# A one-core attention and two-layer feed-forward kernel: the issue order planned with row-weighted TensorE columns and six jittered replays

## The chip, the cores and the metric

The kernel runs on one core of a Trainium2 chip. The metric is the device time of one execution in microseconds (us). The kernel before takes 739.07 us, the median of three executions (737.53, 739.07 and 739.49). One more execution was taken with the hardware profiler on, and all rows below come from that one.

## What is computed

All inputs are float32 (the layer weights reach the kernel as 64-bit floats). The attention has 4 batches, 8 heads, 576 positions and head size 64. Heads 0 to 3 see a local band, heads 4 to 7 a stride of 32:

```
rel = pos[:, None] - pos[None, :]
mask_local = (rel >= 0) & (rel < 32)
mask_strided = (rel >= 0) & (pos[None, :] % 32 == pos[:, None] % 32)
attn = softmax(where(mask, q @ k.T / sqrt(64), -1e9)) @ v
x = attn reshaped to 2304 tokens x 512
h = x @ w_in                              # 512 x 1024
s = h * softmax(h)
x = (s - mean(s)) / sqrt(var(s) + 1e-6) * g_ln @ w_out    # 1024 x 512
out = ((x @ w_a) * (x @ w_b)) @ w_out2    # 512 x 1536, 1536 x 512
```

## The kernel before, in words

**Stages.** The kernel has three kinds of work on the five engines. *Attention*: 40 tiles, 10 for each batch. For a tile TensorE (PE) makes the scores (`scores`, lines 706 and 709), VectorE (DVE) takes the row maxima, subtracts them and sums the exponentials (722, 731, 735, 740), ScalarE (ACT) does the exponential (734), GpSimd (POOL) divides (784), and PE multiplies by V (`pv`, line 803 for batch 0, lines 808 to 810 for the others). `group_T` (line 615) transposes q and k on PE (624). The score products contract over 64 rows of the PE array, the others over 54 to 128. *First layer*: 18 token tiles of 128 (`moe1`, line 838), each 24 matmuls of 512 columns into `h` (861) and then a chain on DVE (854, 866, 869, 890), ACT and POOL; each pair of tiles ends in `s2` (line 903), 96 matmuls of 256 columns into `y` (910). The weights are first converted from 64-bit floats on ACT and DVE (`from_f64`, lines 468, 470, 475, 481) and split into two 16-bit halves (`split_wout`, 548). *Bilinear layer*: from about 330 us on, products of a seven-multiplication scheme into `M` (1288) and output products into `o` (1353). `early` (line 942) converts 12 panels of its weights while attention still runs, and `y_load` (line 1173) normalises and splits the stored tokens on DVE and ACT (1214, 1235, 1240).

**What sets the order.** No engine's order is written out by hand. While the kernel is built, the functions only register items: engine, assumed duration in us, what is read and written, and for PE items a number of columns. Class `Plan` then sorts them, and `emit` issues them in that sequence, so each engine's queue and the DMA queue on SyncE (SP) get one fixed order. `forward` (line 235) is a list scheduler: it simulates the engines with the assumed durations and at each step takes the ready item with the smallest key. `backward` (line 209) runs the same from the end and turns the result into new keys. `schedule` (line 145) repeats backward and forward 120 times with random noise on the keys (seed 4) and keeps the order for which `length` is smallest; `length` is the mean of four replays with the nominal durations, at four phases of the planner's tick.

**The planner's picture of PE's clock.** Both `forward` and `replay` keep a count of columns per planner tick, and an item is taken at twice its duration where the tick before it counted too few:

```
if count[int((at + self.shift) / self.TICK) - 1] < self.ENTRY:
    us *= 2
self.fill(count, at + self.shift, us, o.nbytes)
```

`forward` has one more rule: where the chosen PE item is thin (fewer than `dense` = 1500 columns per us) and the last `span` = 4 us held fewer than `cols` = 5000 columns, it takes a ready dense item instead:

```
if o.nbytes < PARAM["dense"] * us and sum(c for _, c in recent) < PARAM["cols"]:
    many = [x for x in can if x.nbytes >= PARAM["dense"] * x.us]
```

The dense items are the matmuls of the two layers (2048 or more columns each); the thin ones are attention's. The column number of the scores is given on line 713, that of the products with V on line 813 (batch 0) and line 816.

Of the kernel before, what the change touches and what calls it, by code (L numbers as in the profile page):

```python
# [50 lines left out]
NEG = -(2.0 ** 120)  # L51
PASSES = ((0, 0), (0, 1), (1, 0))

PARAM = dict(back=12, first=40, early=(0,), seed=4, noise=0.1, direct=(0,), span=4.0, dense=1500, cols=5000, pf1=(),
             pf2=(), ph1=(), pv=(), pp=(8,), ps1=(), ps2=(), passes=120, e=3,
             PT=3, raw=2, rawl=2, raws=2, qkT=2, V=2, wk=2, xt=1, ln=2, lnT=2, ys=2, raw64=3, f64f=4, att=100.0,
             win=24.5, wout=128.6, moff=-69.7, moe=96.6, conv2=257.2, dconv=15.0, p2=385.0, pre=6.5, fine=(),
             lat=1, plo=(0,), sooner=0.0, soon=(((0, 0), (0, 1), (1, 0), (1, 1)), ((0, 2), (0, 3), (1, 2), (1, 3), (2, 0), (2, 1), (2, 2), (2, 3)), ()), cv=-40.0, dcv=10.0)
# [37 lines left out]
class Plan:  # L96

    TICK, ENTRY = 10.24 / 3, 3060  # L100
    SAME = dict(DVE=0.13, ACT=0.15, POOL=0.05, PE=0.0, CTL=0.0)
    ENGINES = ("PE", "DVE", "ACT", "POOL", "SP", "CTL")

# [36 lines left out]
    def latency(self, a, b):  # L140
        if a.eng == b.eng and a.eng != "SP":
            return self.SAME[a.eng]
        return PARAM["lat"] * (0.28 if a.eng == "PE" else 0.14)

    def schedule(self):

        order, self.shift = self.forward(), 0.0
        best, keys = self.length(order), [o.key for o in self.ops]  # L150
        rnd = random.Random(PARAM["seed"])
        for n in range(PARAM["passes"]):
            if n % PARAM["back"] == 0 and n >= PARAM["first"]:
                for o, key in zip(self.ops, keys):
                    o.key = key
                self.shift = shift
                self.forward()
            self.backward()
            for o in self.ops:
                o.key += rnd.gauss(0.0, PARAM["noise"]) - o.sooner  # L160
            self.shift = self.TICK * (n % 4) / 4
            order = self.forward()
            length = self.length(order)
            if length < best:
                best, keys, shift = length, [o.key for o in self.ops], self.shift
        for o, key in zip(self.ops, keys):
            o.key = key
        self.shift = shift
        order = self.forward()
        self.mean = best  # L170
        return order

    def length(self, order):
        return sum(self.replay(order, self.TICK * (n + 0.5) / 4) for n in range(4)) / 4

    def replay(self, order, shift):
        free = {e: 0.0 for e in self.ENGINES}
        dma = hw = 0.0
        count, start, end = collections.defaultdict(float), {}, {}
        for o in order:  # L180
            e = o.eng
            at = free[e]
            for d in o.deps:
                at = max(at, end[d] + self.latency(d, o))
            for d in o.starts:
                at = max(at, start[d])
            us = o.us
            if e == "PE":
                if count[int((at + shift) / self.TICK) - 1] < self.ENTRY:
                    us *= 2  # L190
                self.fill(count, at + shift, us, o.nbytes)
            start[o] = at
            free[e] = end[o] = at + us
            if e == "SP":
                hw = max(hw, at) + 0.55
                dma = max(dma, hw + 0.65) + o.nbytes / 250e3
                free[e] = max(free[e], hw, dma - 2.0)
                end[o] = dma + 0.75
        return max(end.values())
# [35 lines left out]
    def forward(self):  # L235
        for i, o in enumerate(self.ops):
            o.seq, o.n, o.ready = i, len(o.deps) + len(o.starts), 0.0
            o.outs = []
        for o in self.ops:
            for d in o.deps:  # L240
                d.outs.append((o, True))
            for d in o.starts:
                d.outs.append((o, False))
        free = {e: 0.0 for e in self.ENGINES}
        ready = {e: [o for o in self.ops if o.eng == e and not o.n] for e in self.ENGINES}
        dma = hw = 0.0
        count, recent = collections.defaultdict(float), collections.deque()
        order = []
        for _ in self.ops:
            at, e = min((max(free[e], min(o.ready for o in ready[e])), e) for e in self.ENGINES if ready[e])  # L250
            can = [o for o in ready[e] if o.ready <= at]
            o = min(can, key=lambda o: (o.key, o.seq))
            us = o.us
            if e == "PE":

                while recent and recent[0][0] < at - PARAM["span"]:
                    recent.popleft()
                if o.nbytes < PARAM["dense"] * us and sum(c for _, c in recent) < PARAM["cols"]:
                    many = [x for x in can if x.nbytes >= PARAM["dense"] * x.us]
                    if many:  # L260
                        o = min(many, key=lambda o: (o.key, o.seq))
                        us = o.us
                if count[int((at + self.shift) / self.TICK) - 1] < self.ENTRY:
                    us *= 2
                self.fill(count, at + self.shift, us, o.nbytes)
                recent.append((at + us, o.nbytes))
            ready[e].remove(o)
            o.start, o.took = at, us
            free[e] = o.end = at + us
            if e == "SP":  # L270
                hw = max(hw, at) + 0.55
                dma = max(dma, hw + 0.65) + o.nbytes / 250e3
                free[e] = max(free[e], hw, dma - 2.0)
                o.end = dma + 0.75
            order.append(o)
            for d, full in o.outs:
                lat = self.latency(o, d)
                d.ready = max(d.ready, o.end + lat if full else o.start)
                d.n -= 1
                if not d.n:  # L280
                    ready[d.eng].append(d)
        self.span = max(o.end for o in order)
        return order
# [3 lines left out]
def tile_banded_attention_solu_bilinear(  # L287
# [19 lines left out]
    def pe(us, fn, r, w, cols=60): return P.op("PE", us, fn, r, w, cols)  # L307
# [363 lines left out]
    def att_tile(g, j, fine):  # L671
# [3 lines left out]
        direct = g.b in pm["direct"]  # L675
        i = counter[0]
        counter[0] += 1
        if g.strided:
            ng, nk, W, nx = 2 * NG, RC, 64, S // 2
            cells = [(h, j, (2 * p + h) * RC, half, r, n * NR, h * (S // 2) + a * NR, n * NR, h * (S // 2) + a * NR,  # L680
                      p, 64 * h, (r * 2 + j) * D)
                     for p in reversed(range(NG)) for h in range(2) for half in range(2)
                     for r in (2 * p + half,) if r < len(RUNS) for a, n in (RUNS[r],)]
        else:
            b0, nb = LT[j]
            nm = (nb + 1) // 2
            ng, nk, W, nx = 2 * nm, KB, 128, QB * nb
            cells = [(h, h, m * KB, half, b, QB, QB * b, KB, max(QB * b - ST, 0), h * nm + m, 0, (b * 2 + h) * D)
                     for m in range(nm) for half in range(2) for h in range(2)
                     for b in (b0 + 2 * m + half,) if b < b0 + nb]  # L690
# [9 lines left out]
        def scores():  # L700
# [9 lines left out]
                                 g.T()[w, 1, k0:k0 + kk], start=False, stop=n == last[f, half])  # L710
        pe(ng * nk * 0.42e-3 + sum(0.04 if c[3] else 4 * c[7] / 2.4e3 for c in cells) + 0.03, scores,
           ((g.T, 0), (g.T, 1), "identb", "masks" if g.strided else "maskl"), (sp,),
           ng * nk + sum(c[7] for c in cells))
        mx, e = rings["mx"].new(), rings["e"].new()
        el = ng * nk * 1.25e-3

# [28 lines left out]
        if direct:  # L745
            early = g.b in pm["early"]
# [48 lines left out]
        x = rings["x"].new()  # L795
# [14 lines left out]
                nc.tensor.matmul(o, V[1], pt[0], start=False, stop=True)  # L810
        if direct:
            pe(0.06 + sum(0.045 if c[0] else 4 * c[5] / 2.4e3 for c in cells), pv, (PT, *g.vtoks), (x,),
               sum(2 * c[5] * c[7] / 128 for c in cells))
        else:
            pe(0.06 + sum(0.07 if c[0] else 3 * c[5] / 2.4e3 + 0.01 for c in cells), pv, (PT, *g.V), (x,),
               sum(3 * c[5] * c[7] / 128 for c in cells))
# [140 lines left out]
    order = [groups[b][pr] for b in range(B) for pr in (2, 3, 0, 1)]  # L957
# [7 lines left out]
    def attention(b):  # L965
        P.sooner = pm["sooner"]
        gs = order[4 * b:4 * b + 4]
        ts = batch_tiles(b)
        P.key = pm["att"] * b - pm["pre"]
        for p in (gs[:2], gs[2:]):  # L970
            for g in p:
                load_v(g)
            if b not in pm["direct"]:
                pair_scale(p)
        for n, (g, j) in enumerate(ts):
            P.key = pm["att"] * (b + n / len(ts))
            if not j:
                P.key -= pm["pre"]
                group_T(g)
                if b not in pm["direct"]:  # L980
                    group_v(g)
                load_next()
                P.key += pm["pre"]
            att_tile(g, j, (b * len(ts) + n) in pm["fine"])
        P.sooner = 0.0
# [397 lines left out]
    for ps in range(NP):  # L1383
        for i in range(NSB):
            n = (i + ps) % NSB
# [67 lines left out]
```

## Time and profile before

| | us |
|---|---|
| median of three executions | 739.07 |
| profiled execution, its own time | 744.27 |
| span of its trace, first to last instruction | 742.1 |
| PE busy, DVE busy, ACT busy, POOL busy | 719.9, 519.3, 432.2, 117.2 |
| mean granted TensorE clock, as a share of 2.4 GHz | 0.977 |

The span is the profiled execution without 2.2 us around it. Busy time of PE counts a matmul at whatever clock it was granted, so an engine that is busy all the time can still lose time at half clock. The granted clock is read beside the busy time. A stretch of time, with the busy time of each engine in it, shows which engine could not have done more there.

### The profile page before, as it was taken

Reading aid. Unit: us, or ns where it says so; the run is one execution under the profiler, and the core shown is the slowest. Engines: PE = TensorE matmul, PEld = TensorE weight load, DVE = VectorE, ACT = ScalarE, POOL = GpSimd, SP = SyncE. Lnnn points to the kernel's source line nnn. Section 1 sums busy time; section 2 is a strip of 40 time slices with the busy share of each in tenths; the row PEclk is TensorE's granted clock in tenths of the full one; section 3 lists DMA queues with packets and bytes.
Section 4 is the critical chain, followed back from the end, with each engine's and each line's share of the span. In section 5 each row is a group of like instructions: output and inputs, shape, how many; then the busy total and the mean of one; then the engine's idle time right before and its main releaser. Section 6 shows DMA issues by size and latency. Waiting matters only on the chain.

```text
span 742.1 us, 14124 instructions
## 1 busy us (share of the span) xinstructions
PE 719.9 (97%) x5444; PEld 479.2 (65%) x5444; DVE 519.3 (70%) x1020; ACT 432.2 (58%) x824; POOL 117.2 (16%) x194
## 2 busy tenths in 40 slices
PE   6989889999999999999999999999999999999997
PEld 4867668888787888878655555555555546555553
DVE  4888987858776864898899998547868454434252
ACT  4667977676777876785768666544454333132230
POOL 4441435412433432210000000000000000000000
PEclk9988979999999999999999999999999999999999
DMA  9788996976998585567537034406705031711304
GB/s 212 181 193 222 193 153 136 221 178 160 218 208 165 118 190 141 149 123 254 194 142 272 20 129 129 142 28 187 246 1 170 29 126 44 236 57 46 124 6 165
DMA packets 159327, 109.61 MB, mean 148 GB/s; under 512 B 103702, under 2 KB 137500, under 8 KB 159260
## 3 DMA queue, kind: packets, MB, share of 16 engines
q1 hardware_dynamic: 159260, 108.71, 56.6%
q8 instruction: 43, 0.70, 0.4%
q14 instruction: 24, 0.20, 0.1%
HBM read 65.42 MB, written 27.53 MB: 125 GB/s over the span
## 4 chain that ended last, share of the span: by engine, by line
PE 88%; DVE 6%; ACT 2%; DMA 2%; issue 1%; SPq 0%; POOL 0%; POOLq 0%; DVEq 0%
PE M L1288 31%; PE o L1353 19%; PE y L910 12%; PE h L861 12%; PE s L709 4%; PE s L624 3%; PE xbank L808 2%; PE xbank L803 1%; PE s L706 1%; DMA raw<-in_moe_w_b_dram 1%; PE xbank L810 1%; DMA rawk<-in_k_dram 1%; DMA rawq<-in_q_dram 1%; PE xbank L809 1%; ACT qkT L632 1%
## 5 line engine op out<-in xcount | busy, mean ns | idle before, releaser
L1288 PE MATMUL M<-y,w 128*128 128x384 f16 x1512 | 256.4, 326 | 0.9 <-DVE y L1235 0.6
L1288 PEld LDWEIGHTS <-w 128*128 128x128 f16 x1512 | 147.8, 98 | 102.5 <-issue 1.6
L1353 PE MATMUL o<-wo,p 128*128 128x512 f16 x648 | 147.9, 379 | 0.0
L1353 PEld LDWEIGHTS <-p 128*128 128x128 f16 x648 | 63.3, 98 | 71.0
L910 PE MATMUL y<-lnT,wout 128*128 128x256 f16 x864 | 105.0, 279 | 0.8 <-ACT ys L913 0.6
L910 PEld LDWEIGHTS <-wout 128*128 128x128 f16 x864 | 83.9, 100 | 15.4 <-issue 2.5
L861 PE MATMUL h<-win,xh 128*128 128x512 f32 x288 | 81.5, 422 | 1.4 <-DVE wk L869 1.3
L1295 ACT COPY M<-M 128x384 f32<-128x384 f32 x72 | 33.5, 466 | 68.3 <-PE M L1288 68.2
L861 PEld LDWEIGHTS h<-win,xh 128*128 128x128 f32 x288 | 55.1, 201 | 13.2 <-DVE wk L869 1.1
L1338 ACT ACTIVATE p<-A 128x384 f16<-128x384 f32 x72 | 36.7, 520 | 33.2 <-DVE A L1337 33.1
L1360 DVE SCALAR_TENSOR_TENSOR ob<-o,osc,op 128x512 f32<-128x512 f32 x36 | 27.0, 750 | 40.4 <-PE o L1353 35.1
L1340 DVE SCALAR_TENSOR_TENSOR p<-A,p 128x384 f16<-128x384 f32 x72 | 38.8, 552 | 8.0 <-ACT p L1338 7.7
L709 PE MATMUL s<-qkT 64*54 64x54 f32 (+2 forms) x672 | 38.4, 254 | 2.7 <-ACT qkT L632 2.4
L1299 DVE TENSOR_TENSOR A<-M,V 128x384 f32<-128x384 f32 x36 | 20.0, 555 | 30.0 <-PE M L1288 29.9
L475 DVE SCALAR_TENSOR_TENSOR f64f<-f64f,raw 128x512 int32<-128x512 int32 x52 | 39.4, 762 | 1.4 <-ACT f64f L468 0.7
L866 DVE TENSOR_REDUCE st<-h 128x1 f32<-128x1024 f32 x18 | 22.0, 1221 | 25.9 <-PE h L861 25.9
L861 PE MATMUL h<-win,xl 128*128 128x512 f32 x144 | 40.0, 400 | 0.0
L1337 DVE TENSOR_TENSOR A<-A,M 128x384 f32<-128x384 f32 x36 | 19.9, 552 | 27.0 <-PE M L1288 26.8
L468 ACT ACTIVATE f64f<-raw 128x512 f32<-128x512 f32 x52 | 34.5, 670 | 7.1 <-DMA raw<-in_moe_w_out_dram 2.9
L1310 ACT COPY V<-M 128x384 f32<-128x384 f32 x36 | 17.1, 475 | 34.4 <-PE M L1288 34.3
L709 PEld LDWEIGHTS s<-qkT 64*54 64x54 f32 (+2 forms) x672 | 27.7, 143 | 13.4 <-issue 3.6
L784 POOL TENSOR_TENSOR e<-e,r 128x324 f32<-128x324 f32 (+2 forms) x30 | 26.6, 889 | 59.5 <-DVE r L740 59.5
(170 smaller groups left out, 1135.7 us busy)
## 6 DMA issues: line engine op xcount, KB each, us to landing
raw<-in_moe_w_out_dram SPq DMA_DIRECT2D x20, 512.0 KB
o_scr<-ob SPq DMA_DIRECT2D x36, 256.0 KB
op<-o_scr SPq DMA_DIRECT2D x36, 256.0 KB
raw<-in_moe_w_a_dram SPq DMA_DIRECT2D x12, 512.0 KB
raw<-in_moe_w_b_dram SPq DMA_DIRECT2D x12, 512.0 KB
y_scr<-y SPq DMA_DIRECT2D x14, 384.0 KB
y<-y_scr SPq DMA_DIRECT2D x14, 384.0 KB
y_scr<-ys SPq DMA_DIRECT2D x18, 256.0 KB
```

What stands on the lines that cost most here:

```text
L468: act(0.67, lambda: nc.scalar.activation(f(), raw()[:, :, 1].bitcast(F32), AF.Copy, scale=2.0 ** -112), (raw,), (f,))
L475: nc.vector.scalar_tensor_tensor(fi, fi, 3, raw()[:, :, 0], op0=ALU.logical_shift_left, op1=ALU.bitwise_or)
L709: nc.tensor.matmul(s[64 * half:64 * half + nq, f, col:col + kk], g.T()[w, 0, q0:q0 + nq], g.T()[w, 1, k0:k0 + kk], start=False, stop=n == ...
L784: pool(0.1 + 1.2 * pl, lambda: nc.gpsimd.tensor_tensor(ev(), ev(), r()[:, :ng].unsqueeze(2).to_broadcast([128, ng, nk]), op=ALU.mult), (r, ...
L861: nc.tensor.matmul(h()[:, 512 * n:512 * n + 512], xs[xa]()[:, kk], win[wa][:, kk, 512 * n:512 * n + 512], start=(pi == 0 and kk == 0), sto ...
L910: nc.tensor.matmul(y()[:, 256 * mi:256 * mi + 256], wout[:, kk, wa, 128 * m:128 * m + 128], lnT()[:, xa, kk], start=(pi == 0 and kk == 0), ...
L1288: nc.tensor.matmul(bank()[:, :HB], w()[:, wa, a, kk], y7[b]()[:, xa, kk], start=first and pi == 0 and kk == 0, stop=pi == 2 and kk == 1, s ...
L1295: act(TA, lambda: nc.scalar.copy(dst()[:, :HB], src()[:, :HB]), (src,), (dst,))
L1338: act(TA, lambda x=x, v=v: nc.scalar.activation(v(0), x(), AF.Copy, scale=2.0 ** -PEXP), (x,), ((pu, 0, c, t),))
L1340: dve(TD, lambda x=x, v=v: nc.vector.scalar_tensor_tensor(v(1), x(), 2.0 ** -PEXP, v(0), op0=ALU.mult, op1=ALU.subtract), (x, (pu, 0, c, t ...
L1353: nc.tensor.matmul(o(), pus[u]()[:, xa, c, 128 * tt:128 * tt + 128], wo()[:, 2 * u + c, wa], start=(u == 0 and c == 0 and pi == 0), stop=( ...
L1360: dve(0.75, lambda: nc.vector.scalar_tensor_tensor(ob(), o(), osc()[:, tt:tt + 1], op(), op0=ALU.mult, op1=ALU.add), (o, osc, op), (ob,))
```

## The change

Only numbers and rules of the planner change; no function that issues instructions does, so the kernel after has the same instructions in another order.

- `PARAM` gets `luck=0.06` and `margin=300`; the seed of the search goes from 4 to 1 and its passes from 120 to 100.
- `length` is the mean of six replays (four before), and each replay multiplies every item's duration by a random factor of its own, drawn once around 1.0 with a spread of 6%.
- `replay` and `forward` no longer double a PE item that starts in the first `GRACE` = 40 us of the plan.
- `forward` doubles a PE item where the tick before it counted fewer than `ENTRY` + `margin` columns; `replay` keeps `ENTRY`.
- The columns of a score product (64 rows) count half, and so do those of batch 0's products with V.

```diff
@@ -51,8 +51,8 @@
 NEG = -(2.0 ** 120)
 PASSES = ((0, 0), (0, 1), (1, 0))
 
-PARAM = dict(back=12, first=40, early=(0,), seed=4, noise=0.1, direct=(0,), span=4.0, dense=1500, cols=5000, pf1=(),
-             pf2=(), ph1=(), pv=(), pp=(8,), ps1=(), ps2=(), passes=120, e=3,
+PARAM = dict(luck=0.06, margin=300, back=12, first=40, early=(0,), seed=1, noise=0.1, direct=(0,), span=4.0, dense=1500, cols=5000, pf1=(),
+             pf2=(), ph1=(), pv=(), pp=(8,), ps1=(), ps2=(), passes=100, e=3,
              PT=3, raw=2, rawl=2, raws=2, qkT=2, V=2, wk=2, xt=1, ln=2, lnT=2, ys=2, raw64=3, f64f=4, att=100.0,
              win=24.5, wout=128.6, moff=-69.7, moe=96.6, conv2=257.2, dconv=15.0, p2=385.0, pre=6.5, fine=(),
              lat=1, plo=(0,), sooner=0.0, soon=(((0, 0), (0, 1), (1, 0), (1, 1)), ((0, 2), (0, 3), (1, 2), (1, 3), (2, 0), (2, 1), (2, 2), (2, 3)), ()), cv=-40.0, dcv=10.0)
@@ -97,7 +97,8 @@
 
 
 
-    TICK, ENTRY = 10.24 / 3, 3060
+
+    TICK, ENTRY, GRACE = 10.24 / 3, 3060, 40.0
     SAME = dict(DVE=0.13, ACT=0.15, POOL=0.05, PE=0.0, CTL=0.0)
     ENGINES = ("PE", "DVE", "ACT", "POOL", "SP", "CTL")
 
@@ -146,9 +147,10 @@
 
 
 
+        rnd = random.Random(PARAM["seed"])
+        self.luck = [[rnd.gauss(1.0, PARAM["luck"]) for _ in self.ops] for _ in range(6)]
         order, self.shift = self.forward(), 0.0
         best, keys = self.length(order), [o.key for o in self.ops]
-        rnd = random.Random(PARAM["seed"])
         for n in range(PARAM["passes"]):
             if n % PARAM["back"] == 0 and n >= PARAM["first"]:
                 for o, key in zip(self.ops, keys):
@@ -171,12 +173,14 @@
         return order
 
     def length(self, order):
-        return sum(self.replay(order, self.TICK * (n + 0.5) / 4) for n in range(4)) / 4
-
-    def replay(self, order, shift):
+        return sum(self.replay(order, self.TICK * (n + 0.5) / len(self.luck), x) for n, x in enumerate(self.luck)) / len(self.luck)
+
+    def replay(self, order, shift, luck):
         free = {e: 0.0 for e in self.ENGINES}
         dma = hw = 0.0
         count, start, end = collections.defaultdict(float), {}, {}
+        for o, x in zip(self.ops, luck):
+            o.real = o.us * x
         for o in order:
             e = o.eng
             at = free[e]
@@ -184,9 +188,9 @@
                 at = max(at, end[d] + self.latency(d, o))
             for d in o.starts:
                 at = max(at, start[d])
-            us = o.us
+            us = o.real
             if e == "PE":
-                if count[int((at + shift) / self.TICK) - 1] < self.ENTRY:
+                if at > self.GRACE and count[int((at + shift) / self.TICK) - 1] < self.ENTRY:
                     us *= 2
                 self.fill(count, at + shift, us, o.nbytes)
             start[o] = at
@@ -260,7 +264,7 @@
                     if many:
                         o = min(many, key=lambda o: (o.key, o.seq))
                         us = o.us
-                if count[int((at + self.shift) / self.TICK) - 1] < self.ENTRY:
+                if at > self.GRACE and count[int((at + self.shift) / self.TICK) - 1] < self.ENTRY + PARAM["margin"]:
                     us *= 2
                 self.fill(count, at + self.shift, us, o.nbytes)
                 recent.append((at + us, o.nbytes))
@@ -710,7 +714,7 @@
                                  g.T()[w, 1, k0:k0 + kk], start=False, stop=n == last[f, half])
         pe(ng * nk * 0.42e-3 + sum(0.04 if c[3] else 4 * c[7] / 2.4e3 for c in cells) + 0.03, scores,
            ((g.T, 0), (g.T, 1), "identb", "masks" if g.strided else "maskl"), (sp,),
-           ng * nk + sum(c[7] for c in cells))
+           ng * nk + sum(c[7] for c in cells) / 2)
         mx, e = rings["mx"].new(), rings["e"].new()
         el = ng * nk * 1.25e-3
 
@@ -810,7 +814,7 @@
                 nc.tensor.matmul(o, V[1], pt[0], start=False, stop=True)
         if direct:
             pe(0.06 + sum(0.045 if c[0] else 4 * c[5] / 2.4e3 for c in cells), pv, (PT, *g.vtoks), (x,),
-               sum(2 * c[5] * c[7] / 128 for c in cells))
+               sum(c[5] * c[7] / 128 for c in cells))
         else:
             pe(0.06 + sum(0.07 if c[0] else 3 * c[5] / 2.4e3 + 0.01 for c in cells), pv, (PT, *g.V), (x,),
                sum(3 * c[5] * c[7] / 128 for c in cells))
```

## Rows read from the trace of the kernel before

**Rows 1.** The page: its head, busy time of PE and DVE, granted clock in 40 slices.

```profile
span 742.1 us, 14124 instructions
...
PE 719.9 (97%) x5444; PEld 479.2 (65%) x5444; DVE 519.3 (70%) x1020; ACT 432.2 (58%) x824; POOL 117.2 (16%) x194
...
PEclk9988979999999999999999999999999999999999
```

**Rows 2.** Stretches by stage: us, busy of each engine, granted clock, DMA share, GB/s.

```profile
0.00:20.00 20.00, 12.79 (x103) 9.50 (x103) 9.45 (x22) 8.84 (x13) 8.62 (x28) 1.00 1.05 209
20.00:44.00 24.00, 24.00 (x247) 20.11 (x247) 19.91 (x35) 15.03 (x32) 11.20 (x10) 1.00 0.78 193
44.00:116.00 72.00, 63.34 (x568) 47.76 (x568) 64.47 (x128) 57.88 (x115) 25.78 (x35) 0.81 0.84 178
116.00:200.00 84.00, 84.00 (x937) 68.47 (x937) 61.41 (x113) 60.77 (x113) 30.05 (x44) 0.98 0.87 188
200.00:340.00 140.00, 138.54 (x1348) 112.48 (x1342) 104.59 (x200) 106.55 (x188) 41.55 (x77) 0.99 0.72 164
340.00:440.00 100.00, 99.08 (x592) 57.67 (x590) 92.49 (x192) 68.02 (x127) 0.00 (x0) 1.00 0.47 161
440.00:742.00 302.00, 298.18 (x1670) 163.18 (x1668) 166.97 (x337) 115.06 (x239) 0.00 (x0) 1.00 0.34 109
```

**Rows 3.** The six stretches at about half clock, in the columns of rows 2.

```profile
46.60:53.40 6.80, 6.08 (x39) 4.91 (x40) 6.68 (x12) 5.69 (x14) 3.67 (x3) 0.50 0.95 208
...
63.70:70.50 6.80, 6.80 (x46) 5.54 (x45) 6.80 (x16) 4.89 (x11) 1.00 (x2) 0.50 0.95 239
...
91.00:94.40 3.40, 3.09 (x7) 2.48 (x8) 3.33 (x10) 2.28 (x7) 3.05 (x2) 0.51 1.25 211
...
104.70:114.90 10.20, 7.94 (x69) 5.89 (x69) 9.06 (x19) 7.21 (x14) 4.01 (x6) 0.50 0.44 89
...
166.10:169.50 3.40, 3.40 (x13) 2.75 (x12) 3.13 (x11) 2.16 (x5) 0.20 (x1) 0.51 0.46 141
...
231.00:234.40 3.40, 3.40 (x18) 2.42 (x17) 3.40 (x7) 0.58 (x2) 1.43 (x3) 0.51 0.57 177
```

**Rows 4.** The stretches just ahead of these six falls, in the same columns.

```profile
43.20:46.60 3.40, 1.89 (x32) 1.16 (x30) 3.20 (x7) 1.64 (x4) 0.68 (x1) 1.00 0.23 71
60.20:63.70 3.50, 2.30 (x35) 1.71 (x35) 3.47 (x6) 3.42 (x8) 0.69 (x2) 0.99 0.84 235
87.60:91.00 3.40, 2.12 (x26) 1.41 (x18) 3.11 (x9) 3.40 (x7) 1.12 (x3) 0.99 0.94 200
101.30:104.70 3.40, 3.00 (x82) 2.37 (x81) 2.37 (x5) 2.62 (x5) 0.00 (x0) 0.98 1.33 298
162.70:166.10 3.40, 3.40 (x66) 2.89 (x66) 1.15 (x3) 2.58 (x4) 0.00 (x0) 0.99 0.74 159
227.60:231.00 3.40, 3.40 (x55) 2.65 (x55) 2.73 (x6) 2.88 (x6) 1.11 (x3) 0.98 0.97 231
```

**Rows 5.** Chain that ended last, in order of time: start us, us, what.

```profile
110.43 4.89 PE y L910 x24
116.67 2.73 PE y L910 x24
```

**Rows 6.** Waits of PE from 0 to 20 us: total, times, longest.

```profile
PE s L624 <- DMA rawq<-in_q_dram: 4.7, 1, 4.7
PE s L624 <- ACT qkT L632: 1.2, 1, 1.2
```

**Rows 7.** DVE from 116 to 340 us by line: busy, mean ns, idle before.

```profile
L475 DVE SCALAR_TENSOR_TENSOR f64f<-f64f,raw 128x512 int32<-128x512 int32 x13 | 10.1, 780 | 0.2
L481 DVE SCALAR_TENSOR_TENSOR f64f<-raw,f64f 128x512 int32<-128x512 int32 x13 | 10.0, 773 | 0.1
...
L470 DVE TENSOR_SCALAR raw<-raw 128x512 int32<-128x512 int32 x14 | 6.3, 457 | 0.0
```

## The prediction, made before the changed kernel ran

> **What bounds the kernel now.** I read the page first. TensorE is busy for 719.9 of the 742.1 us of the span, DVE for 519.3, and the granted clock is below full in a few slices of the first third alone [rows 1]. So the kernel is bound by PE, and it can only lose time in two ways: PE stands idle, or it works at 1.2 instead of 2.4 GHz. The stretches by stage put a place to both [rows 2]. Idle time of PE is a stretch less its busy time: 7.2 us in the first 20 us, 8.7 us from 44 to 116 us, 1.5 us from 200 to 340, 0.9 us from 340 to 440, and 3.8 us after 440, all of it behind the last matmul. The stages between have none. The clock is at half in six stretches between 46.6 and 234.4 us, 34.0 us together [rows 3]. PE is busy for 30.7 us of these, so half clock costs 30.7 / 2 = 15.4 us of work at full clock: 12.0 us in the four stretches between 44 and 116 us (23.9 busy), 3.4 us in the two later ones (6.8 busy). That a matmul really takes twice as long there is seen in the chain: 24 matmuls into `y` take 4.89 us at 110 us and 2.73 us at 117 us [rows 5].
>
> The bilinear stage from 340 us on has nothing to win: full clock, and PE busy to within 1% until its last matmul [rows 2]. What the new order can change lies ahead of 340 us. There the stage from 44 to 116 us is not PE's alone: DVE is busy for 64.47 of its 72 us [rows 2]. PE at full clock would need 63.3 - 12.0 = 51.3 us for it, DVE still 64.5. So the half clock of that stage is mostly paid beside DVE, while PE of the two later stretches waits for nothing at all (3.40 of 3.40 us busy) [rows 3].
>
> **The change part by part.** The instructions are the same 14124, so nothing is added or removed; all of it is order, on every engine and on SP's queue.
>
> *Row weights and margin.* A strided score item falls from 1224 to 936 planner columns (648 of the mask, and 576 or half of them, by the code), a local one from 1152 to 768. Both were thin before and stay thin; what changes is that the planner's ticks and the last 4 us of its plan look emptier while attention runs, so a dense item of the first layer is pulled in more often, and orders with long runs of attention are judged slower. The two late falls come right behind such runs: in the 3.4 us ahead of them PE is busy throughout with 66 and 55 small matmuls [rows 4]. The price of the two is 3.4 us, all of it on PE's path. The ends are +3.4 us (both gone) and -3.4 us (two more falls of that kind elsewhere). I take half, a gain of 1.7 us, one fall less: dense work is scarce until `xT` of a batch is complete, so not every run can be broken.
>
> *The stage from 44 to 116 us.* Ahead of its four falls PE was busy for 1.89, 2.30, 2.12 and 3.00 us of about 3.4 [rows 4]: it waited, and then its clock fell. A better mix can save at most what DVE leaves free, 72 - 64.47 = 7.5 us, as long as DVE's work of the stage stays there. The row for what DVE can reach over a long stretch is that from 340 to 440 us, 92.49 of 100 us with PE at 99% [rows 2]. At that share the stage would take 64.47 / 0.925 = 69.7 us, a gain of 2.3 us. Some of DVE's work can also go earlier: from 20 to 44 us DVE is busy for 19.91 of 24 us, and 0.925 of 24 is 22.2, room for 2.3 us more. The 40 us of grace bear on just that: the plan before took PE's first items at double length, and PE's granted clock was 1.00 up to 44 us [rows 2], so the plan was late there and now no longer is. I take 2.3 + 2.3 = 4.6 us; the ends are 7.5 us and nothing.
>
> *The first 20 us.* PE waits 4.7 us for the first load of q, which no order can shorten, and 1.2 us for ACT once [rows 6]. The rest of the 7.2 us is at most 2.5 us to win. The DMA engines have a share of 1.05 in that stretch [rows 2], so a load that is moved ahead pushes another back; one such wait could cost as much as the first, 4.7 us. I take 0, between ends of different sign.
>
> *Small idle times.* 1.5 and 0.9 us from 200 to 440 us [rows 2] may go or be replaced; I take 0, with an end at a gain of 2.4 us.
>
> *Six replays with durations off by 6%, seed, passes.* They cost nothing on the chip; they choose another order. An order that was best over durations that are a little wrong should lose less to waits that the plan did not see, and these are the waits of the 44 to 116 us stage, which is counted already. I add nothing.
>
> Sum: 1.7 + 4.6 = 6.3 us. The profiled execution took 744.27 us, 5.2 us above the median and above all three other times, so a part of its losses may be that run's own. I take the gain off the median: 739.07 - 6.3 = 732.8 us. All the best ends together are 3.4 + 7.5 + 2.5 + 2.4 = 15.8 us, or 723.3 us.
>
> **A rule weighed.** Four of six falls came behind stretches in which PE stood idle for part of the time, two behind stretches in which it did not [rows 4]. The Trainium skill, "TensorE: Matmul & The Clock Gate", section "Why this matters for your kernels", names idle gaps of PE between bursts of matmuls as the cause of a mid-kernel drop, and says nothing of how many rows a matmul uses. By that rule alone the row weights would steer nothing, and the sum would lose its 1.7 us; the trace agrees with it in four cases and differs in two.
>
> **The rivals.** *No change (within 0.3%, 2.2 us, about what a measurement of this kernel can tell from no change).* Either the weights steer nothing, as by idle time alone, or falls only change places: with DVE at 90% of the 44 to 116 us stage, PE there must wait for DVE somewhere, and behind each wait the clock can fall. For it: all four of these falls have DVE busy for 2.37 to 3.47 us of the 3.4 ahead [rows 4]. Against it: the two late falls, and DVE's slack from 116 to 200 us (61.41 of 84) [rows 2], to which work could move. It gives 739.1 us.
>
> *Slower: DVE's work is pushed past 340 us.* If the plan pulls first-layer tiles forward to fill PE, their chains on DVE come first, and weight conversions, which are due late, are put off. One converted panel is 780 + 773 + 457 ns, 2.0 us of DVE [rows 7]. From 340 to 440 us DVE has only 7.5 us free [rows 2], and PE waits there for the operands that DVE splits. From the fourth panel on that goes past 340 us each costs PE 2.0 us. With eight put off, 16.1 - 7.5 = 8.6 us are lost: 739.1 + 8.6 = 747.7 us, and 744.3 us if both late falls are cured as well. For it: DVE is the tightest engine beside PE there. Against it: from 116 to 340 us DVE is busy for only 166.0 of 224 us, so there is room for both.
>
> **How the numbers follow.** The case in which PE's half-clock and waiting time ahead of 340 us shrink has 0.58: both losses that the change aims at are in the rows, and no instruction is added. It runs from 723.3 to 736.9 us. No change has 0.17, since an order that is drawn anew on all engines seldom lands within 2.2 us. Slower has 0.25, with 741.3 to about 750 us. The range from 724 to 748 us leaves out the last part of the best ends and eight panels or more put off, together some 0.15. The forecast's own range is 724 to 737 us.
>
> **What would show it.** Right: less than 25 us at half clock where there were 34.0, none of it after 150 us behind a stretch in which PE was fully busy; the work of the 44 to 116 us stage done some 4 to 5 us sooner, with DVE above 92% in it; the bilinear stage as long as before. Wrong: as many us at half clock in other places (no change); PE idle for more than 3 us between 330 and 440 us, with DVE the releaser (slower); or a first stage longer by a wait for a load. If the time falls by much more than 7 us, DVE's work has left the 44 to 116 us stage, and my bound on it was wrong.

## The result, and the profile after

The kernel after takes 749.89 us (747.77 to 751.33, four executions), the kernel before 738.75 us beside it. The ratio is 1.015, with a 95% interval from 1.0121 to 1.0179: 11.1 us slower. I had forecast 732.8 us, with a range up to 748.0.

The page of the kernel after, its head, busy times and granted clock:

```profile
span 747.7 us, 14093 instructions
...
PE 719.5 (96%) x5444; PEld 479.1 (64%) x5444; DVE 519.5 (69%) x1020; ACT 430.6 (58%) x824; POOL 119.2 (16%) x194
...
PEclk9757689999999999999999999999999999999999
```

The five engines work through as many instructions as before [rows 1]. The total is 14093, not "the same 14124", so the 31 lie outside of the engines' work. PE is busy as long as before, and the span is 5.6 us longer. So PE stands idle for 747.7 - 719.5 = 28.2 us, where it was 742.1 - 719.9 = 22.2 us.

The whole difference is there before the first layer starts. The first `h` matmul, before and then after (start us, us):

```profile
51.23 2.08 PE L861 MATMUL h<-win,xh 128*128 128x512 f32 x4
```

```profile
57.50 2.07 PE L865 MATMUL h<-win,xh 128*128 128x512 f32 x4
```

It comes 6.3 us later, and what follows takes 690.2 us where it took 690.9. The stretches by stage (columns as in [rows 2]):

```profile
0.00:20.00 20.00, 12.44 (x101) 8.98 (x102) 9.85 (x22) 8.03 (x11) 8.99 (x28) 1.00 0.88 180
20.00:44.00 24.00, 19.70 (x193) 15.56 (x193) 14.94 (x31) 12.28 (x27) 8.39 (x7) 0.70 0.70 164
44.00:116.00 72.00, 63.85 (x515) 48.33 (x515) 59.20 (x115) 54.83 (x110) 24.23 (x33) 0.74 0.79 177
116.00:200.00 84.00, 83.61 (x979) 68.89 (x980) 66.66 (x122) 65.39 (x123) 29.94 (x46) 1.00 0.94 199
200.00:340.00 140.00, 137.17 (x1366) 112.18 (x1365) 106.76 (x199) 104.74 (x187) 47.67 (x80) 1.00 0.70 153
340.00:440.00 100.00, 98.95 (x609) 59.37 (x607) 90.19 (x189) 66.70 (x126) 0.00 (x0) 1.00 0.50 173
440.00:748.00 308.00, 303.75 (x1697) 165.83 (x1694) 171.94 (x348) 118.64 (x245) 0.00 (x0) 1.00 0.34 110
```

Against [rows 2], PE idles 4.3 us from 20 to 44 us where it had no gap, and DVE does 14.94 us of work there instead of 19.91. From 44 to 116 us PE is busy about as long, and DVE does 5.3 us less; some 10 us of its work have moved past 116 us. The late falls are gone: after 108.5 us the clock stays full. But it is at half from 30.0 to 60.6 us, and three times more up to 108.5 us (stretches of the kernel after, same columns):

```profile
30.00:60.60 30.60, 27.37 (x247) 21.12 (x248) 20.27 (x41) 16.55 (x38) 14.77 (x14) 0.50 0.55 144
...
70.90:77.70 6.80, 6.34 (x16) 5.01 (x17) 5.39 (x12) 4.73 (x10) 0.19 (x1) 0.52 0.54 151
...
84.60:94.80 10.20, 10.11 (x64) 7.67 (x65) 7.32 (x14) 9.01 (x22) 3.56 (x7) 0.52 0.81 174
...
105.10:108.50 3.40, 3.40 (x11) 2.58 (x10) 3.39 (x5) 3.40 (x6) 0.24 (x2) 0.55 1.22 222
```

That is 51.0 us where [rows 3] had 34.0. It isn't the whole account, because **the clock column can't be read at the start.** It says 1.00 there in both kernels. The durations of one form of matmul say otherwise. First two rows: the kernel before, score matmuls from 0 to 27 and from 72 to 90 us. Then its 64x96 scores from 30 to 43 and from 43.2 to 46.6 us:

```profile
L709 PE MATMUL s<-qkT 64*54 64x54 f32 x80 | 7.3, 300 | 1.2 <-ACT qkT L632 0.8 <-ACT sm L739 0.3
...
L709 PE MATMUL s<-qkT 64*54 64x54 f32 x40 | 2.4, 218 | 0.0
...
L709 PE MATMUL s<-qkT 64*64 64x96 f32 x32 | 1.8, 378 | 0.0
...
L709 PE MATMUL s<-qkT 64*64 64x96 f32 x20 | 0.9, 258 | 0.0
```

So before ran at half clock (1.2 GHz) for its first 43 us, and the kernel after for about 26 us: its transposes of q took 1.19 us for six at 5.8 us and 0.71 us at 26.4 us, when the clock had risen. Three and a half us later it fell again. With the start counted, both profiled executions have about 77 us of half clock (43.2 + 34.0, some 26 + 51.0), and the 5.6 us between these two are idle time of PE.

The longest wait of PE behind its first, in the chain that ended last of the kernel after (start us, us, what):

```profile
26.44 0.66 PE s L628 x6
...
27.18 0.65 ACT qkT L639
27.83 0.56 ACT f64f L472
28.39 0.14 ACT PT L785
...
28.64 0.64 ACT win L500
29.28 0.43 ACT e L738
...
29.73 0.55 DVE sm L739
30.28 1.01 DVE f64f L485
...
31.32 0.63 ACT win L500
31.94 0.88 PE y L773 x3
```

And PE's waits up to 62 us in the kernel after:

```profile
PE s L628 <- POOL maskl L420: 5.8, 1, 5.8
PE y L773 <- ACT win L500: 3.9, 1, 3.9
```

The second row names the release that came last by the profile. By the names of the tiles, PE waits for POOL's division (L777, written to `lnT`), which ends just before PE goes on. Rows of DVE, POOL and PE (start us, us, what, idle time before it):

```profile
28.73 0.17 DVE L744 RECIPROCAL r<-sm 128x6 f32<-128x6 f32 x1
...
29.35 1.38 POOL L501 TENSOR_TENSOR win<-f64f,win 128x512 fp32r<-128x512 f32 x1 [1.90 <-ACT win L500]
30.70 1.17 POOL L777 TENSOR_TENSOR lnT<-e,r 128x324 f32<-128x324 f32 x1
...
31.93 0.90 PE L773 MATMUL y<-ident,lnT 128*128 128x128 f32 x3 [3.87 <-ACT win L500]
```

To be read as: each engine goes through its items in the plan's order, and weight conversion stands ahead of attention twice. The sum that the reciprocal (L744) needs is ready at 26.56 us, but on DVE a piece of a conversion is running and four more items go first, two of them conversion too, and it starts 2.2 us later. The division could follow at 28.9 us, but on POOL the subtraction of a conversion (L501) goes first and itself waits for ACT (L500), so it starts 1.8 us later. Together that is about the whole wait. On ACT the copy of the late transposes (L639), itself waiting for PE, puts that conversion off by some 0.6 us more. The first products with V stand behind this wait in PE's queue. They come at 33.7 us, where before had them at 21.5 us, and V's loads are issued until 31.7 us, not 23.2; the wait is 3.87 of these 12 us, and in most of the rest PE works at items that the plan put ahead of them. Rows of the matmuls and loads of `raws`, before and then after (min/median/max ns, first and last start):

```profile
L803 PE MATMUL xbank<-PT,raws x72: 267/310/352, 21.5 to 35.4; 54*64 54x54 f32 x60, 18*64 18x18 f32 x12
L591 SPq DMA_DIRECT2D raws<-in_v_dram x12: 287/332/764, 2.8 to 23.2; - x12
```

```profile
L807 PE MATMUL xbank<-PT,raws x24: 268/310/348, 33.7 to 36.0; 54*64 54x54 f32 x20, 18*64 18x18 f32 x4
L595 SPq DMA_DIRECT2D raws<-in_v_dram x12: 273/328/1608, 2.8 to 31.7; - x12
```

### The profile page after: what moved, and what is told of

The parts are those of the page before. It is cut to its first block, busy times and chain, and to the rows that moved or that the text cites. A ratio compares the mean times of both kernels' runs of the same rounds, so it can differ in the third digit from the quotient of the medians.

```text
span 747.7 us, 14093 instructions
## 1 busy us (share of the span) xinstructions
PE 719.5 (96%) x5444; PEld 479.1 (64%) x5444; DVE 519.5 (69%) x1020; ACT 430.6 (58%) x824; POOL 119.2 (16%) x194
## 4 chain that ended last, share of the span: by engine, by line
PE 88%; DVE 4%; ACT 3%; DMA 3%; issue 1%; SPq 0%; POOL 0%; POOLq 0%; DVEq 0%; ACTq 0%
PE M L1292 32%; PE o L1357 18%; PE h L865 12%; PE y L914 12%; PE s L713 4%; DMA raw<-in_moe_w_out_dram 2%; PE s L628 2%; PE xbank L812 2%; PE xbank L807 1%; PE s L710 1%; PE y L773 1%; ACT qkT L636 1%; PE xbank L814 1%; DMA rawk<-in_k_dram 1%; PE xbank L813 1%
## 5 line engine op out<-in xcount | busy, mean ns | idle before, releaser
L914 PE MATMUL y<-lnT,wout 128*128 128x256 f16 x864 | 101.1, 273 | 3.1 <-ACT ys L917 3.0
L914 PEld LDWEIGHTS <-wout 128*128 128x128 f16 x864 | 82.2, 98 | 16.1 <-issue 5.5
L1342 ACT ACTIVATE p<-A 128x384 f16<-128x384 f32 x72 | 36.8, 521 | 31.7 <-DVE A L1341 31.5
L865 PE MATMUL h<-win,xl 128*128 128x512 f32 x144 | 41.6, 413 | 0.0
L479 DVE SCALAR_TENSOR_TENSOR f64f<-f64f,raw 128x512 int32<-128x512 int32 x52 | 37.0, 717 | 2.4 <-ACT f64f L472 1.4
L726 DVE TENSOR_REDUCE mx<-s 128x6 f32<-128x324 f32 (+2 forms) x40 | 19.2, 484 | 23.0 <-PE s L713 22.9
L796 POOL TENSOR_TENSOR P<-e,P 128x324 f16<-128x324 f32 (+2 forms) x30 | 29.2, 980 | 24.6 <-ACT P L795 24.6
```

The source lines that it names most:

```text
L479: nc.vector.scalar_tensor_tensor(fi, fi, 3, raw()[:, :, 0], op0=ALU.logical_shift_left, op1=ALU.bitwise_or)
L796: pool(0.15 + 1.4 * pl, lambda: nc.gpsimd.tensor_tensor(plo, ev(), ph, op=ALU.subtract), (e, ("P2", pi, 0)), (("P2", pi, 1),))
L865: nc.tensor.matmul(h()[:, 512 * n:512 * n + 512], xs[xa]()[:, kk], win[wa][:, kk, 512 * n:512 * n + 512], start=(pi == 0 and kk == 0), sto ...
L914: nc.tensor.matmul(y()[:, 256 * mi:256 * mi + 256], wout[:, kk, wa, 128 * m:128 * m + 128], lnT()[:, xa, kk], start=(pi == 0 and kk == 0), ...
L1342: act(TA, lambda x=x, v=v: nc.scalar.activation(v(0), x(), AF.Copy, scale=2.0 ** -PEXP), (x,), ((pu, 0, c, t),))
```

## The experiments

Theories: **A**, the 40 us without doubling (the grace) give the head of the program a wrong order; **B**, the row weights and the margin mix the layers badly later; **C**, it is only another draw of a noisy search.

**The grace alone, in the kernel before** (and the same condition in `forward`).

```
+    TICK, ENTRY, GRACE = 10.24 / 3, 3060, 40.0
-                if count[int((at + shift) / self.TICK) - 1] < self.ENTRY:
+                if at > self.GRACE and count[int((at + shift) / self.TICK) - 1] < self.ENTRY:
```

> The kernel before with one part of the change alone: no PE item is doubled in the first 40 us of the plan (seed 4, 120 passes, old columns, four nominal replays). Theory A (PE really starts at half clock: 64x54 score matmuls take 300 ns up to 27 us in both traces and 218 ns later, so a plan that leaves the doubling out puts the first 40 us in a wrong order): slower than before by 5 us or more, 744 to 755 us. Theory B (row weights and margin pull first-layer work ahead of attention's chains): within 3 us of before, 736 to 742 us. Theory C (only another draw of the search): anywhere from 734 to 750, with no long half-clock stretch that is special to the first 60 us.

Measured: 751.91 us, ratio 1.0155 (1.0127 to 1.0183). The first products with V come at 31.3 us, and V's loads go on until 33.1 us:

```profile
L803 PE MATMUL xbank<-PT,raws x24: 267/310/352, 31.3 to 33.5; 54*64 54x54 f32 x20, 18*64 18x18 f32 x4
L591 SPq DMA_DIRECT2D raws<-in_v_dram x12: 286/340/683, 1.7 to 33.1; - x12
```

One part, same seed as before, all of the loss, and a head that is late alike: the first `h` matmul starts at 57.2 us. The wait of 3.87 us isn't what the two have in common: PE's longest behind the first load is 1.9 us here, up to 62 us.

**All but the grace, in the kernel after.**

```
-    TICK, ENTRY, GRACE = 10.24 / 3, 3060, 40.0
+    TICK, ENTRY, GRACE = 10.24 / 3, 3060, 0.0
```

> The kernel after with the grace set to 0 us and all other parts kept (seed 1, 100 passes, row weights, margin, six jittered replays). Theory A: most of the 11 us comes back, 736 to 745 us, and PE waits for less than 3 us between 20 and 44 us (4.3 us in the kernel after). Theory B: stays at 747 us or more. Theory C: anywhere from 735 to 750.

Measured: 739.58 us, ratio 1.0006 (0.9988 to 1.0024). From 20 to 44 us PE idles 0.5 us, not 4.3, and DVE does 21.89 us of work; the first `h` matmul starts at 51.5 us:

```profile
20.00:44.00 24.00, 23.50 (x229) 19.26 (x229) 21.89 (x39) 15.91 (x33) 11.56 (x10) 1.00 0.76 195
```

```profile
L807 PE MATMUL xbank<-PT,raws x62: 267/310/352, 21.4 to 36.0; 54*64 54x54 f32 x50, 18*64 18x18 f32 x12
L595 SPq DMA_DIRECT2D raws<-in_v_dram x12: 321/347/1054, 2.3 to 24.7; - x12
```

So the other parts alone, the row weights and the margin among them, cost nothing at this seed, and theory B falls. The half clock at the start lasts longer here than in the kernel after, which is slower. Six transposes take twice as long at 49.7 us as at 57.7 us, with the column at 1.00:

```profile
49.69 1.17 PE L628 MATMUL s<-ident,rawq 96*128 96x96 f32 x6
...
57.67 0.66 PE L628 MATMUL s<-ident,rawk 96*128 96x96 f32 x6
```

**The two heads exchanged.** Each order written out as a list of item numbers, taken from the two plans:

```
-    emit(tc, P.schedule(), stacks)
+    emit(tc, [P.ops[i] for i in ORDER], stacks)
```

> The reverse splice: the 218 items that the plan after starts in its first 45 us, in its order, then all others in the order of before. Theory A: as slow as after, 746 to 752 us. Theory B: as fast as before, 737 to 741 us.

Measured: 750.76 us, ratio 1.0141 (1.0115 to 1.0168). With the first 218 of 2891 items of the kernel after, the order of before is as slow as the kernel after, and the first `h` matmul starts at 58.1 us. How much of that is the head and how much the joint isn't settled: the reverse shows that a joint can cost some us too.

> A written-out order: the 199 items (of 2891) that the plan before starts in its first 45 us, in the order of before, then all others in the order of after. Theory A: the loss sits in the head, so 736 to 743 us. Theory B: the loss sits in how the layers are mixed later, so 747 to 751 us. Theory C: both ends possible, and the reverse splice need not mirror it.

Measured: 745.69 us, ratio 1.0085 (1.0058 to 1.0111). The reverse gives back about two fifths; it falls between the two expectations, with the first `h` matmul at 53.7 us behind before's own head. Perhaps the rest of after's order suits only its own head; no run shows that.

**Before once more**, unchanged:

> The kernel before, unchanged, for a second profile: the first one (744.27 us) was 5 us above its median. Theory A: a time near 739 us, the first product with V at about 21 us and the first h matmul at about 51 us as in the first profile, and less than 77 us of half clock (43.2 us at the start, where matmul durations show it though the column reads 1.00, and 34.1 us in six recorded stretches). Theory C: those milestones differ by several us between two executions of one kernel.

Measured: 741.42 us, once, span 739.2 us, first products with V at 21.1 us and first `h` matmul at 49.5 us. By durations and the column it ran at half clock for some 64 us (some 27 at the start and 37.4 in six stretches), not 77. So one order is granted different clocks in two executions, with 2.9 us between their spans. That is a part of why two single profiles show 5.6 us where medians show 11.1. Against this second profile the kernel after is 8.5 us longer: PE is idle for 4.0 us more (28.2 against 24.2) and busy for 4.5 us more. So the loss is not idle time alone.

**More work for PE at the start**, to make the plan's full clock true.

```
+    junk = []
+    def warm(n):
+        if not junk:
+            nc.vector.memset(wout[:, 8], 0.0)
+            junk.append(handles["psL"][0].tile([128, FF1], F32, tag="h", name="h", bufs=1))
+        for i in range(n):
+            nc.tensor.matmul(junk[0][:, :512], wout[:, 8, 0, :128], wout[:, 8, 1], start=True, stop=True)
...
+    order = [Warm(16)] + order
```

> The kernel after, in its own order, with 16 matmuls of 128x512 on zeros in front of PE's first item, into a PSUM tile that is not in use yet; their output is not used. They run while PE waits for its first load (5.8 us). If the clock column is right (1.00 from the start), the transposes of q keep their 375 ns and the 64x54 score matmuls their 300 ns, and the time is 749 to 753 us. If PE really starts at half clock (theory A), these fall to about 247 and 218 ns behind the extra work, for as long as attention's small matmuls hold the clock, and the time falls by 0 to 5 us, 745 to 750 us.

Measured: 749.35 us, ratio 1.0131 (1.0111 to 1.015). Transposes of this kernel up to 10 us, and from 10 to 20 us:

```profile
L628 PE MATMUL s<-ident,rawq 96*128 96x96 f32 x6 | 0.7, 245 | 0.0
...
L628 PE MATMUL s<-ident,rawq 96*128 96x96 f32 x6 | 1.2, 376 | 0.0
```

245 ns behind 16 dense matmuls, 376 again a little later: the start without them is at half clock, and attention's small matmuls didn't hold the full one here. The time hardly moves.

> As the run with 16 matmuls in front, and 3 more of them (128x512 on zeros) behind every PE item that the plan starts in its first 40 us, so that the plan's assumption of full clock there is made true by extra work. Theory A: the transposes take 247 ns and the scores 218 ns in most of the first 40 us, the first product with V comes earlier than 33.7 us, and the time falls to 738 to 746 us, less what the extra matmuls cost PE (about 0.65 us for each item at full clock). If the half clock at the start is no cause: 750 us or more, by the extra work.

Measured: 752.1 us, ratio 1.0179 (1.0156 to 1.0201), not theory A's 738 to 746 us but the other branch. Now the transposes from 20 to 27 us are at full clock too, and PE's wait for ACT and POOL is still there:

```profile
L628 PE MATMUL s<-ident,rawq 96*128 96x96 f32 x12 | 1.3, 245 | 0.0
```

The row of that wait, among PE's waits up to 62 us:

```profile
PE y L773 <- ACT win L500: 3.1, 1, 3.1
```

> The kernel after with the 16 matmuls in front and one, not three, behind each PE item of the plan's first 45 us. With three, PE ran at full clock up to 31.9 us, yet each item took as long with its extra work as at half clock without. If the half clock between 30 and 61 us is what makes this head slow, one filler (about 0.25 us an item) leaves PE ahead: first h matmul before 55 us (57.5 in the kernel after), 741 to 747 us. If the head is slow by its order on the other queues, whatever PE's clock: PE waits 3 us or more for ACT and POOL near 28 us as before, first product with V after 32 us, and 748 to 752 us.

Measured: 749.79 us in three executions (a fourth took 759.14), ratio 1.012 (1.0099 to 1.0141): the wait is 4.0 us, the first products with V come at 34.8 us, and the first `h` matmul starts at 56.1 us. That is the expectation's branch of the other queues. The clock fell twice before 27 us, as one filler is too little there, but from 30.0 to 60.6 us, where the kernel after has 0.50 throughout, it was nearly full in both runs (three fillers, then one):

```profile
30.00:60.60 30.60, 27.18 (x287) 17.12 (x288) 18.34 (x36) 15.24 (x36) 13.16 (x11) 0.94 0.53 136
```

```profile
30.00:60.60 30.60, 26.66 (x276) 18.34 (x276) 22.30 (x43) 17.43 (x40) 17.22 (x14) 0.89 0.58 162
```

So with most of this half clock gone the kernel is as slow, which speaks against the clock there as the cause. It is not settled whether this head would do at a full clock that costs nothing, since the fillers took PE's time: with three, the late transposes start at 26.5 us, as in the kernel after (26.4).

> The kernel before, in its own order, with the same 16 matmuls in front and one behind each PE item of the plan's first 45 us. PE is busy from 20 to 44 us without a gap in before, at half clock by its matmul durations. If half clock binds there, the first h matmul comes 2 to 5 us earlier than 49.5 to 51.2 us and the time is 734 to 738 us; if other engines bind as closely, it stays within 738 to 742 us.

Measured: 740.61 us, ratio 1.0013 (0.9993 to 1.0034), first `h` matmul at 51.7 us: the branch in which other engines bind as closely, and nothing gained.

**Other draws of the search.**

```
-... seed=1, noise=0.1, ...
+... seed=3, noise=0.1, ...
```

> The kernel after with another draw of the search (seed 3), grace kept. Theory A (the grace spoils the head, whatever the draw): 745 us or more, first h matmul after 55 us. Theory C (seed 1 was an unlucky draw): 735 to 745 us, first h matmul near 51 us.

Measured: 751.34 us, ratio 1.0144 (1.012 to 1.0167), first products with V at 25.5 us, first `h` matmul at 53.1 us. As slow as seed 1, though the `h` milestone was missed by 2 us: its head is less late, and it loses more behind (two late falls, at 160 and 215 us).

> The kernel after without the grace, seed 4. Theory A: no slower than 745 us, first h matmul near 51 us. Together with seeds 1 (739.6 us) and 8 (745.0 us) it gives the spread of draws without the grace; if row weights, margin and jitter help in themselves, the three should lie below before (739.4 us) on the mean, and they do not if this one is above 734 us.

Measured: 742.81 us, ratio 1.0038 (1.0002 to 1.0074).

> The kernel after without the grace, with another draw of the search (seed 8, 200 passes in place of seed 1 and 100). Theory A: as fast as before or a little faster, 733 to 741 us, as nothing of the head is planned wrongly. Theory C (the draw alone decides): anywhere from 735 to 752 us. If row weights, margin and jitter are worth something in themselves, it lies below 738 us.

Measured: 745.03 us, ratio 1.0077 (1.0058 to 1.0096): not the gain that theory A expected, and well outside its numbers. Its search also had 200 passes.

> The kernel before with another draw of its search (seed 1, nothing else changed). If the draw alone moves the time by several us, it lies between 739 and 748 us, with the first h matmul near 51 us. If before's planner gives 739 us whatever the seed, 737 to 741 us.

Measured: 745.07 us, ratio 1.0072 (1.0053 to 1.0091).

> As seed 1, with seed 3: 739 to 748 us if draws differ. If the mean of seeds 1, 3 and 5 is above the 742.5 us of the three kernels without the grace (739.6, 742.8, 745.0), row weights, margin and jitter are worth something; if it is at or below, they are not.

Measured: 744.55 us, ratio 1.0064 (1.004 to 1.0087).

> As seed 1, with seed 5: 739 to 748 us if draws differ; no draw without the grace reaches the 749.9 us of the kernel after.

Measured: 745.95 us, ratio 1.0089 (1.006 to 1.0118).

Side by side: three plans with the grace take 749.9, 751.3 and 751.9 us. Three of the kernel after without it take 739.6, 742.8 and 745.0 us, mean 742.5. Before's planner at seeds 4, 1, 3 and 5 takes 739.4, 745.1, 744.6 and 745.9 us, mean 743.8. A draw moves the time by 6 us, and by medians no draw without the grace is as slow as one with it. The first `h` matmul says the same: it starts at 57.5, 53.1 and 57.2 us with the grace, and between 49.5 and 52.2 us in all profiles of the seven without. Row weights, margin, jitter and passes together are worth 1.3 us between these means, which draws of this spread can't tell from nothing. No version here beats before; without the grace, the kernel after is its equal at seed 1, and slower at the two other seeds.

## Why the prediction was wrong

The step that failed is the second half of the term for the stage from 44 to 116 us: "The 40 us of grace bear on just that: the plan before took PE's first items at double length, and PE's granted clock was 1.00 up to 44 us [rows 2], so the plan was late there and now no longer is." I took the column at its word. The durations in the same trace (300 against 218 ns) contradict it, and I had used that very test for [rows 5]. To take these items at double length fitted the chip; the grace took that away, and a part that I counted as 2.3 us of gain costs 10.3 us at seed 1 (749.9 against 739.6) and 12.5 us at seed 4 (751.9 against 739.4).

The same reading left the start out of the price of half clock. PE was busy for 36.0 of the first 43.2 us, so by the same halving up to 18.0 us of work at full clock went there, more than the 15.4 us that I counted (columns of [rows 2]):

```profile
0.00:43.20 43.20, 35.99 (x331) 29.10 (x332) 28.66 (x54) 23.38 (x43) 19.15 (x38) 1.00 0.90 201
```

Point by point:

- **Row weights, 1.7 us.** The two late falls did go, and at 3.4 us they were sized as their rows say. But the weights are not shown to be the cause: the same weights at seed 8 and at seed 3 leave falls at 151 and 226 us, and at 160 and 215 us. Of the five plans with the new weights three have no fall from 117 us to the last matmul, and all five without them have one; that leans towards the weights, but other parts changed with them and draws differ.
- **The stage from 44 to 116 us, 4.6 us.** DVE did not go above 92% there; it fell from 64.47 to 59.20 us of 72. Its work did not move ahead of 44 us but away from there (14.94 us instead of 19.91).
- **The first 20 us, taken as 0.** PE starts 1.1 us later (5.8 us of wait instead of 4.7), inside the bound of 4.7 us. The row names POOL, but loads of V are queued in front of q's, whose two loads are issued at 1.67 and 3.63 us, not at 0.72 and 1.73; that these ended the wait is inferred.
- **Replays, seed and passes, "they cost nothing on the chip".** True of instructions, wrong of the time. Before was one draw of a search, and a good one: three others of the same planner are 5 to 6.5 us slower. I measured the change from a lucky draw and gave the new draw no price. In this result the draw happened to cost nothing, as seed 1 without the grace is level with before.
- **The slower rival.** The sign was in it, the mechanism was not, and that its upper end of about 750 us lies at the measured time is chance. DVE is busy for 90.19 us from 340 to 440 us (92.49 before), and PE waits 1.05 us there. Nothing was pushed past 340 us that mattered.
- **No change, by idle time alone.** The long fall at 30.0 us came within PE's idle 3.87 us, which fits the rule that I weighed; but before shows falls without idle time [rows 4], and its longest gap of PE past 20 us is 2.1 us. So neither is the whole story.

What stays open: why the search chooses late heads when the doubling is dropped, as the wait of 3.87 us behind blocked queues is in one of the plans with the grace and none of that length in the first 62 us of the other two; and whether such a head would be good at a full clock that costs PE nothing.

## What to carry to other kernels

Before a planner's picture of a stretch is corrected, hold it against durations of one instruction form inside and outside of that stretch; a column that reads full may only be empty there. A plan drawn by a noisy search is one sample: compare planners over several seeds, and put each rule in alone, since one wrong rule hid among five here. And look at when the first item of the next stage starts, and at the queues of the head: in the kernel after, 6.3 us lost ahead of the first `h` matmul were never made good.

## What the runs showed of the hardware that I had not expected

The granted clock reads 1.00 at the start while matmuls take their half-clock durations, for 26 to 60 us in the profiles without added matmuls; in the kernel before with the grace, six transposes take 1.17 us at 30.2 us and 0.66 us only at 62.3 us, with the column at 1.00 for both. Behind sixteen 128x512 matmuls on zeros the transposes take 245 ns, not 375, at 6 us, and 376 ns again at 12.9 us, after attention's small matmuls. And two executions of one unchanged order differed by some 12 us in their time at half clock.
